# Top-k attention and an MLP on one core: the scores of the first batch one item further ahead and at another place of the slot

## The chip, the cores and the metric

The kernel runs on one core of a Trainium2 chip. The time is that of the device, in microseconds (us), from the first to the last instruction and what lies around them; the lower the better. PE is the matrix engine, DVE the vector engine, ACT the scalar engine, POOL the general one; SP issues DMAs. Each engine works through its own list of instructions in the order in which the program gave them out, and waits for others by semaphores.

## The reference, cut to what matters

```python
# q, k, v: (8, 8, 576, 64)  batch, heads, sequence, head size
scores = (1 / np.sqrt(64)) * q @ k.transpose(0, 1, 3, 2)
kth = np.partition(scores, -32, axis=-1)[..., -32:-31]     # the 32nd largest of a row
scores = np.where(scores >= kth, scores, -1e9)
p = np.exp(scores - scores.max(-1, keepdims=True))
x = (p / (p.sum(-1, keepdims=True) + 1e-9)) @ v            # -> (4608, 512)
h = x @ w_in                                               # (512, 2048)
y = gelu_exact(h) @ w_out                                  # (2048, 512)
```

## The kernel before, in words

**Items.** The attention is cut into items. An item is 128 query rows of two heads of one batch ("pair"), that is two rows of 576 scores in each of 128 partitions; two short items per batch take the last 64 queries of two pairs each. There are 144 items. The first 16 (`EARLY`) are the full tiles of batch 0, ordered so that four items (one tile of all four pairs) complete 128 tokens; batch 0 is "the first batch".

**Slots.** The program is written out by hand, with no scheduler: slot `n` gives out instructions for several items at different stages. Slots 0 to 17 are made by `early_slot(n)`, those from 18 on by the loop behind it. Before the slots come the transposes of pairs 0 to 2 with the scores of items 0 and 1. In slot `n` of `early_slot` there is, in the order in which it is given out:

- POOL adds the two halves of one block of weights (`weights_add`, L231). The weights arrive as 64-bit numbers, in 16 blocks, one per slot, and are turned into 32-bit ones in the kernel: ACT reads the high part in the middle of the slot before (`weights_size(u, 0)`, L211), ACT goes on with it at that slot's end (`weights_size(u, 1)`, L214, for the first blocks also L220; for the later ones DVE does that last step, L216).
- DVE compares the two halves of the rows of item n+1 (`larger`, L416); it is the first step of the top-k search and marks a slot's start on DVE below.
- `scores(n + 2)`: PE multiplies queries and keys: the last 64 keys into a bank of their own (`t_ps`, L343, or L357 for a short item), the 512 others into a tile of two banks (`s_ps`, L380 or L395). ACT scales and copies both to SBUF (L351 or L363, and L388 or L400).
- `attend(n - 2)`: PE multiplies the probabilities by the values (`o`, L638), ACT copies the product to `xT` (L656), PE spreads the reciprocals of the sums over the other half of the same bank (L651), and DVE multiplies `xT` by them (`copy_x`, L657).
- `top_k(n)`: DVE finds the 32nd largest of each row in six rounds of MAX8 and MATCH_REPLACE8. Rounds are given out in two parts, and `copy_x` stands between them: behind two rounds in the slots where a tile of 128 tokens is completed (`whole`), behind three in the others.
- `softmax(n - 1)`, twice, once per row: ACT L506 and L507.
- `transposes(n - 1)`: PE turns the probabilities over into a tile of two banks (`tp`, L568) and the last keys into another bank (`tp_t`, L542); ACT copies both (`pt`, L594 and L552).
- transposes of queries and keys of a later pair (`prep`, L291, copied by ACT in L296).
- `mlp(k)`: up to k pieces of the matmuls of the MLP are strewn between these. A piece is eight matmuls of `x @ w_in` (L721) or one of `g @ w_out` (L813), and every slot has a number of pieces (`left`); before slot 5 there are none, and dummy matmuls (`keep_busy`, L1092) stand there.
- At the end: `smaller` and `add_small` (POOL), `run_ends`, the rest of the search, `weights_size(u, 1)`, `run_gelus` (ACT, with a change of its table, L741), `threshold` (POOL, L486 and L487), `sum_up`.

`run_ends` copies a finished tile of y out of PSUM (L822) and stores it by a DMA of ACT's queue. It is so for the first five tiles of tokens only (`full_piece`).

**PSUM.** The eight banks are given out by tags. The tag that matters here is `pr`, two banks and one buffer: the scores and the transposed probabilities take turns in it. The two calls that do so:

```python
s_ps = pair_tile("s_ps", "l1" if second else "pr")      # in scores()
pr[0] = pair_tile("tp")                                 # in transposes(), tag "pr"
```

Of the kernel before, what the change touches and what calls it, by code (L numbers as in the profile page):

```python
# [14 lines left out]
def kernel(  # L15
# [30 lines left out]
    NP = H // 2  # L46
# [106 lines left out]
    EARLY = NP * NM  # L153
# [109 lines left out]
    def bank(name):  # L263

        tags = ("z",) if few[0] else ("z", "y2") if begun[0] else ("z", "y0", "y1", "y2")
        tag = tags[turn[0] % len(tags)]
        turn[0] += 1
        return ps.tile([P, 512], f32, tag=tag, bufs=1, name=name)
# [50 lines left out]
    def row(i, e):  # L319
        return S_of[i][:, e * S : (e + 1) * S]  # L320

    def spread(t, step, n):

        return bass.AP(tensor=t.tensor, offset=t.offset, ap=[list(t.ap[0]), [step, 2], [1, n]])

    def half(r, e):


        return slice((r ^ e) * TL, ((r ^ e) + 1) * TL)
# [5 lines left out]
    def pair_tile(name, tag="pr"):  # L335
        return ps.tile([P, 2, 512], f32, tag=tag, bufs=1, name=name)
# [31 lines left out]
    def scores(i, second=False):  # L368
        if i >= N or i in S_of:
            return  # L370
        pair, t = items[i]
        S_of[i] = s = work.tile([P, 2 * S], f32, tag="s", bufs=6, name="s")
        s_ps = pair_tile("s_ps", "l1" if second else "pr")
        if not few[0]:
            last_keys(i, bank("t_ps"))()
        if t < NM:
            q_t, kt = q_of[pair][:, t * P : (t + 1) * P], kt_of[pair]
            for e in range(2):
                rows = slice(e * D, (e + 1) * D)
                nc.tensor.matmul(  # L380
                    s_ps[:, e], lhsT=q_t[rows, :], rhs=kt[rows, 0:SM], start=True, stop=True
                )
            if i == 0:

                nc.scalar.activation(s[:, 0:SM], s_ps[:, 0], func=AF.Copy, scale=scale)
                nc.scalar.activation(s[:, S + TL :], s_ps[:, 1], func=AF.Copy, scale=scale)
                return
            nc.scalar.activation(spread(s, S + TL, SM), s_ps, func=AF.Copy, scale=scale)  # L388
        else:

            for r in range(2):
                kt = kt_of[pair + r]
                for e in range(2):
                    rows = slice(e * D, (e + 1) * D)
                    nc.tensor.matmul(  # L395
                        s_ps[half(r, e), r, :], lhsT=kt[rows, SM + P + e * TL : SM + P + (e + 1) * TL],
                        rhs=kt[rows, 0:SM], start=True, stop=True,
                    )
            s2 = s.rearrange("p (r n) -> p r n", r=2)
            nc.scalar.activation(s2[:, :, 0:SM], s_ps, func=AF.Copy, scale=scale)  # L400
# [4 lines left out]
    def paired(i):  # L405

        return PAIRED <= i < N and i not in SINGLE
# [19 lines left out]
    def smaller(i):  # L427

        if paired(i):
            both, top = lists_of[i][:, 1].bitcast(i32), lists_of[i][:, 0].bitcast(i32)  # L430
            nc.gpsimd.tensor_tensor(both, both, top, op=ALU.subtract)  # L431
# [63 lines left out]
    def add_small(i):  # L495
        if i < 0 or i >= N:
            return
        st = stat_of[i]
        nc.gpsimd.tensor_scalar(st["den"], st["den"], 1e-9, None, op0=ALU.add)  # L499

    def softmax(i, e):

        if i < 0 or i >= N:
            return
        st, s = stat_of[i], row(i, e)
        nc.scalar.activation(s, s, func=AF.Prelu, bias=st["neg"][:, e : e + 1], scale=1.0, alpha=STEEP)  # L506
        nc.scalar.activation(  # L507
            s, s, func=AF.Exp, bias=st["bias"][:, e : e + 1], scale=1.0,
            accum_out=st["den"][:, e : e + 1],
        )  # L510
# [94 lines left out]
    def copy_x():  # L605
        while copies:
            copies.pop()()
# [83 lines left out]
    for base in range(0, NT, RING):  # L691
        whole = [(0, 256), (256, 256)] if base else [(t * P, P) for t in range(NM)]
# [317 lines left out]
    def run_gelus():  # L1010
        while waiting:
            u = waiting.pop(0)
            if u in HELD:
                gelus(u - 2)
            gelus(u)
            if eager[0]:
                run_small(9)

    def run_ends():
        while ends:  # L1020
            ends.pop(0)()
# [23 lines left out]
    def mlp(n):  # L1045
        for _ in range(n):
            if done[0] >= len(pieces) or pieces[done[0]][0] > ready[0] or left[0] <= 0:
                return
            if not all(w in (known[0] or made) for w in pieces[done[0]][1]):
                return  # L1050
            pieces[done[0]][2]()
            done[0] += 1
            left[0] -= 1
            if eager[0]:
                run_gelus()
                run_small(9)
# [38 lines left out]
    for pair in range(3):  # L1095
        for piece in transpose_qk(pair, pair == 0):
            piece()
        if pair < 2:
            scores(pair)


    slots_of = [
# [33 lines left out]
    def early_slot(n):  # L1136

        left[0] = room_in(n) if n >= FIRST else 0
        begun[0] = n >= FIRST
        known[0] = set(made)  # L1140
        weights_add(unit_in(n))
        larger(n + 1)
        scores(n + 2)
        product = attend(n - 2)
        mlp(1)
        while dividing:
            dividing.pop()()
        searches = top_k(n, lambda: inverse(n - 1))
        whole = n - 2 < EARLY and (n - 1) % NP == 0
        for _ in range(2 if whole else 3):  # L1150
            next(searches)
        copy_x()
        ready[0] = n_tok[0]
        softmax(n - 1, 0)
        softmax(n - 1, 1)
        u = unit_in(n + 1)
        if u is not None:
            weights_size(u, 0)
        mlp(2)
        if n < FIRST:  # L1160
            keep_busy(6 if product else 12, ident)
        prep = prep_in.pop(n, [])
        for piece in prep[:1]:
            piece(None)
        tr = transposes(n - 1) if n - 1 < EARLY else []
        for x, piece in enumerate(tr):
            piece()
            if x == len(tr) - 1:
                known[0] = None
            mlp(1)  # L1170
        known[0] = None
        for piece in prep[1:]:
            piece(None)
            mlp(1)
        if n < FIRST:
            keep_busy(8, ident)
        smaller(n + 1)
        add_small(n - 1)
        mlp(left[0])
        run_ends()  # L1180
        for _ in searches:
            pass
        if u is not None:
            weights_size(u, 1)
        run_gelus()
        threshold(n)
        normalise(n - 1)
        sum_up(n + 2)
        run_small(6)
        next_loads(n)  # L1190
# [5 lines left out]
    for n in range(LAST_EARLY + 1, ahead):  # L1196

        left[0] = room_in(n)
        few[0] = n > START + 2
        eager[0] = n > N  # L1200
        larger(n + 1)
        for piece in squares_in.pop(n, []):
            piece()
        two = n >= SPREAD[1] and n % 2 == 0 and n + 3 < N and items[n + 3][1] < NM
        scores(n + 2, two)
        if two:
            scores(n + 3)
        product = attend(n - 3) if n - 3 >= EARLY else False
        copy_x()
        mlp(1)  # L1210
        if n % 2:
            run_gelus()
        tr = transposes(n - 2)
        if product and done[0] < len(pieces) and pieces[done[0]][0] > ready[0]:

            for piece in tr[:1]:
                piece(n + 2)
            tr, ready[0] = tr[1:], n_tok[0]
        mlp(1)
        softmax(n - 1, 0)  # L1220
        if n % 2:
            mlp(ODD)
        mlp(1)
        prep = prep_in.pop(n, [])
        for x, piece in enumerate(tr + prep[:1]):
            piece(n + 2)
            ready[0] = n_tok[0]
            if x == 2:
                break
            mlp(1)  # L1230
        ready[0] = n_tok[0]
        softmax(n - 1, 1)
        smaller(n + 1)
        add_small(n - 1)
        for piece in prep[1:]:
            piece(None)
            mlp(1)

        run_gelus()
        mlp(left[0])  # L1240
        run_ends()
        run_gelus()
        if n < N:
            for _ in top_k(n, lambda: inverse(n - 1)):
                pass
        else:
            inverse(n - 1)
        threshold(n)
        normalise(n - 1)
        sum_up(n + 2)  # L1250
        if n in sums_in:
            weight_sums(sums_in[n])
        run_small(6)
# [38 lines left out]
```

## Time and profile before

| | |
|---|---|
| median of 3 runs | 1562.04 us (1559.5 to 1562.1) |
| the profiled execution, its own time | 1561.84 us |
| its span, first to last instruction | 1559.1 us |
| PE busy | 1514.1 us, 97% |
| DVE busy | 1336.6 us, 86% |
| ACT busy | 1157.0 us, 74% |
| POOL busy | 1095.8 us, 70% |
| the chain that ended last | PE 72%, DVE 7%, POOL 6%, ACT 2% |

The shares are means over a span with different stages. The stage that the change touches, slots 0 to 17, ends at about 201 us of the span; what happens in it is read from windows and from the instructions in order of time, where a row gives start, duration, engine, line, and in brackets the idle time of the engine ahead of the instruction with what ended it. Two instructions of ACT that follow each other overlap a little, so the time that one takes out of ACT's day is best read from its start to the start of the next.

### The profile page before, as it was taken

To read this page: it belongs to the slowest core of one execution; us is meant where nothing else is said; L and a number is where in the kernel's file an instruction comes from. 1 tells how busy PE (TensorE), PEld (TensorE's weight loads), DVE (VectorE), ACT (ScalarE), POOL (GpSimd) and SP (SyncE) were. 2 spreads that over 40 slices of the span, in tenths; PEclk is the share of its full clock that TensorE was granted. 3 is DMA by queue.
4 is the path that set the end of the run, shared out by engine and by line. 5 is a ranking of instruction groups with operands and counts; after the bars stand their busy time and mean duration, and the time that the engine had idled before them with its cause. 6 is when DMAs were issued, how large, how long until landed. Compare 5 with 4: busy or idle time off the path is not lost.

```text
span 1559.1 us, 28536 instructions
## 1 busy us (share of the span) xinstructions
PE 1514.1 (97%) x9478; PEld 1178.0 (76%) x9478; DVE 1336.6 (86%) x4605; ACT 1157.0 (74%) x2030; POOL 1095.8 (70%) x1253
## 2 busy tenths in 40 slices
PE   8888999999999999999999999999999999999998
PEld 6765666667777778887777778788777777787887
DVE  8988889899989998998989997988998998888700
ACT  6988867677777777777777777777777778787720
POOL 4664555556687878776787877777778786876732
PEclk9999999999999999999999999999999999999999
DMA  6523210022101111011200111002210111000000
GB/s 178 159 84 104 85 39 8 8 38 39 24 14 26 36 31 30 1 30 38 39 23 16 30 32 45 1 17 38 37 24 19 28 30 32 15 1 15 8 14 14
DMA packets 184243, 56.37 MB, mean 36 GB/s; under 512 B 175008, under 2 KB 175584, under 8 KB 184096
## 3 DMA queue, kind: packets, MB, share of 16 engines
q1 hardware_dynamic: 180720, 52.23, 14.2%
q10 hardware_dynamic: 3152, 2.00, 0.4%
q8 instruction: 74, 1.21, 0.3%
q14 instruction: 73, 0.60, 0.1%
q0 software_dynamic: 224, 0.33, 0.1%
HBM read 45.08 MB, written 9.44 MB: 35 GB/s over the span
## 4 chain that ended last, share of the span: by engine, by line
PE 72%; DVE 7%; POOL 6%; ACT 2%; issue 1%; DVEq 0%; POOLq 0%
PE h_ps L721 26%; PE y_ps L874 15%; PE o L638 7%; PE tp L568 6%; PE s_ps L380 6%; PE y_ps L813 3%; PE seven L872 2%; DVE top L460 2%; POOL s L518 2%; DVE rest L463 2%; PE tp_t L343 1%; PE y_ps L836 1%; PE y_ps L839 1%; PE o L667 1%; PE tp_t L542 1%
## 5 line engine op out<-in xcount | busy, mean ns | idle before, releaser
L721 PE MATMUL h_ps<-xT,w_in_sb 128*128 128x256 f32 (+1 forms) x2688 | 529.3, 347 | 0.0
L721 PEld LDWEIGHTS h_ps<-xT,w_in_sb 128*128 128x128 f32 x2688 | 433.5, 191 | 64.6 <-issue 24.6
L460 DVE MAX8 top<-lists 128x8 f32<-128x288 f32 x798 | 323.6, 447 | 0.0
L518 POOL TENSOR_TENSOR s<-s,rden 128x1152 f32<-128x1152 f32 x128 | 269.1, 2102 | 0.3 <-DVE rden L493 0.3
L507 ACT ACTIVATE s<-s,bias 128x576 f32<-128x576 f32 x288 | 223.4, 776 | 12.0
L463 DVE MATCH_REPLACE8 lists<-top,lists 128x288 f32<-128x288 f32 x532 | 231.5, 443 | 0.0
L506 ACT ACTIVATE s<-s,neg 128x576 f32<-128x576 f32 x288 | 225.7, 784 | 4.0 <-POOL neg L486 4.0
L460 DVE MAX8 low<-lists 128x8 f32<-128x288 f32 x532 | 214.7, 445 | 0.0
L499 POOL TENSOR_SCALAR den<-den 128x2 f32<-128x2 f32 x144 | 31.4, 218 | 259.2 <-ACT s L507 255.4
L584 ACT COPY pt<-tp 128x1024 f32<-128x1024 f32 x128 | 130.0, 1016 | 101.8 <-PE tp L568 101.8
L431 POOL TENSOR_TENSOR lists<-lists 128x576 int32<-128x576 int32 x133 | 187.6, 1411 | 4.4
L423 POOL TENSOR_TENSOR lists<-s 128x576 int32<-128x576 int32 x133 | 187.0, 1406 | 0.0
L568 PE MATMUL tp<-ident,s 128*128 128x128 f32 x1152 | 152.7, 273 | 9.8 <-ACT s L507 9.8
L486 POOL TENSOR_SCALAR neg<-kth 128x2 f32<-128x2 f32 x133 | 84.9, 639 | 106.4 <-DVE kth L477 106.4
L638 PEld LDWEIGHTS o<-pt,raw_v 128*64 128x64 f32 x1440 | 93.0, 137 | 87.0 <-issue 45.3
L568 PEld LDWEIGHTS tp<-ident,s 128*128 128x128 f32 x1152 | 134.0, 141 | 28.9 <-ACT s L507 13.1
L638 PE MATMUL o<-pt,raw_v 128*64 128x256 f32 (+1 forms) x1440 | 154.7, 361 | 0.0
L388 ACT ACTIVATE s<-s_ps 128x1024 f32<-128x1024 f32 x127 | 124.9, 1026 | 22.5 <-PE s_ps L380 21.6
L380 PE MATMUL s_ps<-kt,qm 64*128 64x512 f32 x512 | 131.9, 625 | 4.3 <-ACT pt L584 2.9
L874 PE MATMUL y_ps<-w_out_sb,sum 128*128 128x256 f32 x448 | 133.3, 379 | 0.0
L493 DVE RECIPROCAL rden<-den 128x2 f32<-128x2 f32 x144 | 23.0, 160 | 120.8 <-POOL den L499 120.0
L463 DVE MATCH_REPLACE8 lists<-low,lists 128x288 f32<-128x288 f32 x266 | 115.8, 443 | 0.0
(168 smaller groups left out, 2744.8 us busy)
## 6 DMA issues: line engine op xcount, KB each, us to landing
raw_v<-in_v_dram SPq DMA_DIRECT2D x64, 128.0 KB, 2.3
w_out_sb<-in_moe_w_in_dram SPq DMA_DIRECT2D x14, 511.8 KB, 4.8
out_dram<-late SPq DMA_DIRECT2D x26, 256.0 KB, 2.1
raw_q<-in_q_dram SPq DMA_DIRECT2D x96, 64.0 KB, 2.0
raw_k<-in_k_dram SPq DMA_DIRECT2D x96, 64.0 KB, 2.0
w_out_sb<-in_moe_w_out_dram SPq DMA_DIRECT2D x10, 511.8 KB, 4.2
w_sum<-in_moe_w_out_dram SPq DMA_DIRECT2D x4, 511.8 KB, 5.6
raw_q<-in_q_dram SPq DMA_DIRECT2D x96, 8.0 KB, 1.8
```

The costliest lines, as they stand in the source:

```text
L380: nc.tensor.matmul(s_ps[:, e], lhsT=q_t[rows, :], rhs=kt[rows, 0:SM], start=True, stop=True)
L423: nc.gpsimd.tensor_tensor(t[:, 1].bitcast(i32), a.bitcast(i32), b.bitcast(i32), op=ALU.add)
L431: nc.gpsimd.tensor_tensor(both, both, top, op=ALU.subtract)
L460: nc.vector.max(x[:, e], src[:, e])
L463: nc.vector.match_replace(dst[:, e], x[:, e], src[:, e], LOWEST)
L506: nc.scalar.activation(s, s, func=AF.Prelu, bias=st["neg"][:, e : e + 1], scale=1.0, alpha=STEEP)
L507: nc.scalar.activation(s, s, func=AF.Exp, bias=st["bias"][:, e : e + 1], scale=1.0, accum_out=st["den"][:, e : e + 1],)
L518: nc.gpsimd.tensor_tensor(s, s, wide, op=ALU.mult)
L568: nc.tensor.transpose(tp[:, j * P : (j + 1) * P], s[:, first + j * P : first + (j + 1) * P], ident)
L638: nc.tensor.matmul(o[e * D : (e + 1) * D, 0:n], lhsT=vt[:, j, e, :], rhs=pt[:, e * NM + j if j < NM else 2 * NM, x], start=(j == 0), stop= ...
L721: nc.tensor.matmul(h_tile(u)[:, i, :], lhsT=w_in_sb[:, ko, f * P : (f + 1) * P], rhs=xT[:, ko, c0 : c0 + n], start=(ko == 0), stop=(ko == ...
L874: nc.tensor.matmul(acc[names][:, k], lhsT=lhsT, rhs=rhs, start=(j == 0 and k == 0), stop=(j == FT // 2 - 1 and k == 1),)
```

## The change

The scores are made one item further ahead and are given out late in the slot. `scores(2)` is given out before slot 0, and slot `n` makes `scores(n + 3)` behind the transposes and the pieces between them, instead of `scores(n + 2)` at the slot's head. `smaller` and `add_small` with one piece of the MLP stand ahead of it; in slots 0 to 4 the second run of dummy matmuls stands behind it. `copy_x` stands behind two rounds of the search in all early slots. `run_ends` moves from the end of the slot to behind the second softmax, in the early slots and in the main loop.

```diff
@@ before the slots
     for pair in range(3):
         for piece in transpose_qk(pair, pair == 0):
             piece()
-        if pair < 2:
-            scores(pair)
+        scores(pair)
@@ early_slot(n)
         larger(n + 1)
-        scores(n + 2)
         product = attend(n - 2)
         mlp(1)
         while dividing:
             dividing.pop()()
         searches = top_k(n, lambda: inverse(n - 1))
-        whole = n - 2 < EARLY and (n - 1) % NP == 0
-        for _ in range(2 if whole else 3):
+        for _ in range(2):
             next(searches)
         copy_x()
         ready[0] = n_tok[0]
         softmax(n - 1, 0)
         softmax(n - 1, 1)
+        run_ends()
         u = unit_in(n + 1)
         if u is not None:
             weights_size(u, 0)
...
         for piece in prep[1:]:
             piece(None)
             mlp(1)
+        smaller(n + 1)
+        add_small(n - 1)
+        mlp(1)
+        if n + 3 <= EARLY + 3:
+            scores(n + 3)
         if n < FIRST:
             keep_busy(8, ident)
-        smaller(n + 1)
-        add_small(n - 1)
         mlp(left[0])
-        run_ends()
         for _ in searches:
             pass
         if u is not None:
             weights_size(u, 1)
@@ the main loop
         ready[0] = n_tok[0]
         softmax(n - 1, 1)
+        run_ends()
         smaller(n + 1)
...
         run_gelus()
         mlp(left[0])
-        run_ends()
         run_gelus()
```

## The prediction

> **What bounds the kernel now.** I read the windows first, to see which engine is full in the stage that the change touches, then the instructions in order of time through that stage, and last the waits. In the windows the columns are the stretch, its length, the busy time of PE, weight loads, DVE, ACT and POOL, then the granted clock, the DMA share and GB/s.
>
> ```profile
> 40.00:60.00 20.00, 17.32 (x158) 13.38 (x159) 19.93 (x74) 19.77 (x32) 14.27 (x16) 1.00 0.57 161
> 80.00:100.00 20.00, 14.62 (x118) 10.24 (x114) 19.31 (x70) 17.55 (x28) 13.67 (x13) 0.91 0.28 106
> 140.00:160.00 20.00, 20.00 (x115) 10.24 (x113) 16.11 (x59) 16.80 (x28) 10.71 (x11) 0.96 0.18 43
> ```
>
> There are two stages. Up to about 100 us DVE is full, and between 40 and 60 ACT is too (19.77 of 20); PE has room, and part of its work there is dummy matmuls. From about 140 us on PE is full. Every later slot has its fixed share of MLP pieces and PE stays full, so a microsecond that slots 0 to 17 lose or win should reach the end whole. Here is ACT from slot 2 to slot 3, from one copy of `xT` to the next, and the starts of two slots on DVE:
>
> ```profile
> 34.16 0.24 ACT L656 COPY xT<-o 128x128 f32<-128x128 f32 x1
> ...
> 39.53 0.27 ACT L552 COPY pt<-tp_t 128x128 f32<-128x128 f32 x1
> 39.68 1.26 ACT L214 ACTIVATE w_in_sb<-w_sum,low 128x1024 int32<-128x1024 f32 x1
> 40.82 1.19 ACT L220 ACTIVATE w_sum<-w_sum 128x1024 int32<-128x1024 uint32 x1
> 41.87 0.29 ACT L351 ACTIVATE s<-t_ps 128x128 f32<-128x128 f32 x1
> 42.02 1.05 ACT L388 ACTIVATE s<-s_ps 128x1024 f32<-128x1024 f32 x1
> 42.93 0.30 ACT L656 COPY xT<-o 128x128 f32<-128x128 f32 x1
> ```
> ```profile
> 39.44 0.75 DVE L416 TENSOR_TENSOR lists<-s 128x576 f32<-128x576 f32 x1
> ...
> 48.49 0.75 DVE L416 TENSOR_TENSOR lists<-s 128x576 f32<-128x576 f32 x1
> ```
>
> ACT's round takes 42.93 − 34.16 = 8.77 us, and no row of it has a bracket, that is, ACT never waits; DVE's takes 48.49 − 39.44 = 9.05. ACT has 0.28 us to spare per slot. What the change does to ACT's list decides.
>
> **What the order of the lists becomes.** On PE almost nothing changes. The scores of item n+3 are given out at the end of slot n instead of at the head of slot n+1, and from slot 9 on the 6 or 7 pieces of a slot are all used up ahead of the new place: 1 + 2 before the transposes, 3 in them, 1 new. PE meets the scores where it met them before. In slots 0 to 4 they swap places with the dummy matmuls; in slots 5, 6 and 8, where the pieces wait for their weights, they pass one or two. POOL's and SP's lists keep their order: the scores issue no DMA, and `smaller` and `add_small` pass nothing of POOL's. `scores(2)` ahead of slot 0 is the old order too. These edits cost nothing by themselves.
>
> On ACT, however, the copies of the scores (L351, L388) pass `weights_size(u, 1)` (L214, in the first slots also L220) and the gelus. L388 needs `s_ps`, and `s_ps` lies in the buffer that L594 empties:
>
> ```profile
> 86.28 0.99 ACT L594 COPY pt<-tp 128x1024 f32<-128x1024 f32 x1
> 87.18 0.27 ACT L552 COPY pt<-tp_t 128x128 f32<-128x128 f32 x1
> 87.33 2.08 PE L380 MATMUL s_ps<-kt,qm 64*128 64x512 f32 x4 [1.04 <-ACT pt L594]
> ```
> ```profile
> 146.76 1.13 PE L380 MATMUL s_ps<-kt,qm 64*128 64x512 f32 x4
> ...
> 147.94 1.03 ACT L388 ACTIVATE s<-s_ps 128x1024 f32<-128x1024 f32 x1 [0.79 <-PE s_ps L380]
> ...
> 150.12 0.44 PE L651 MATMUL o<-ident,rden 128*64 128x128 f32 x4
> ```
>
> PE can start `s_ps` 0.15 us after ACT goes on from L594 (87.33 − 87.18), and L388 starts 1.18 us behind that (147.94 − 146.76). Before, L214 and L220 filled this time. After, only L552 and L351 do, 0.15 us each from start to start (39.68 − 39.53, 42.02 − 41.87).
>
> *Slots 1 to 4.* ACT newly waits 0.15 + 1.18 − 0.30 = 1.03 us per slot. Its round becomes 9.80 us, over DVE's 9.05, so ACT takes over as the bound: **4 × 1.03 = 4.1 us**. If DVE's round is taken as the old bound it is 4 × 0.75 = 3.0. I take the first, for ACT's hand-over to DVE was just in time when the MLP begins in slot 5: PE waits for ACT, and is done at 60.94 + 0.44 = 61.38 for DVE's L657 at 61.49.
>
> ```profile
> 60.59 0.30 ACT L656 COPY xT<-o 128x128 f32<-128x128 f32 x1
> ...
> 60.94 0.44 PE L651 MATMUL o<-ident,rden 128*64 128x128 f32 x4 [0.55 <-ACT xT L656]
> ...
> 61.49 0.29 DVE L657 TENSOR_TENSOR xT<-xT,o 128x128 f32<-128x128 f32 x1
> ```
>
> *Slot 0.* Item 3 needs the queries of its pair, which ACT copies at 21.59:
>
> ```profile
> 11.35 0.63 ACT L296 COPY qm<-tp_qk 128x512 f32<-128x512 f32 x1
> ...
> 13.63 1.02 ACT L388 ACTIVATE s<-s_ps 128x1024 f32<-128x1024 f32 x1 [0.79 <-PE s_ps L380]
> 21.59 0.60 ACT L296 COPY qm<-tp_qk 128x512 f32<-128x512 f32 x1
> ...
> 25.50 0.77 ACT L506 ACTIVATE s<-s,neg 128x576 f32<-128x576 f32 x1
> ```
>
> From such a copy to L388 it took 13.63 − 11.35 = 2.28, so L388 falls at 23.87. Behind it come its own 0.91 (42.93 − 42.02), then L214 and L220, 41.87 − 39.68 = 2.19, and the first softmax starts at 26.97 instead of 25.50: **1.5 us**.
>
> *Slots 5 to 7.* Where PE has pieces, ACT waited for `s_ps` already, as the 0.79 at 147.94 shows. The new wait of 1.03 replaces such a wait in part; I take 0.4 each, **1.2 us**, from −0.8 (one old wait goes and nothing comes) to 3.1 (all of it is new).
>
> *The three slots that end in gelus (8, 11, 15).*
>
> ```profile
> 97.04 0.26 ACT L552 COPY pt<-tp_t 128x128 f32<-128x128 f32 x1
> ...
> 102.77 0.33 ACT L656 COPY xT<-o 128x128 f32<-128x128 f32 x1
> ```
>
> ACT now takes 102.77 − 97.04 = 5.73 us from L552 to L656, for L214, a table load, four gelus and the two copies of the scores, without a wait. The new order has the same instructions and the wait of 1.03 ahead of L388. PE and DVE wait for this L656 already, so **3 × 1.0 = 3.1 us** (1.5 to 5.0; PE's pieces and the transposes of a pair can hold the scores up longer).
>
> *The other slots with pieces and a block of weights (9, 10, 12, 13, 14).* PE is full, and the question is whether ACT has L656 ready when PE comes to L651. L388 at 147.94, its 0.91, then L214's 1.14 (40.82 − 39.68) put L656 at 149.99; L651 follows by 0.35 (60.94 − 60.59), at 150.34 instead of 150.12: **5 × 0.2 = 1.0 us** (0 to 2.5).
>
> *The rest.* `copy_x` one round of the search earlier makes DVE wait at L657 instead of working on. ACT's round being the longer one, DVE stands later against ACT once, not in every slot, and the biases of the next softmax are still early: nothing. The copy of y now stands behind the softmaxes with its DMA issue; what it passes on ACT are copies that wait for PE anyway, and the next tile in its bank is two slots away: nothing, a few tenths either way.
>
> The sum is 4.1 + 1.5 + 1.2 + 3.1 + 1.0 = 10.9 us; with the bounds, 3.0 + 1.5 − 0.8 + 1.5 + 0 = 5.2 to 4.1 + 1.5 + 3.1 + 5.0 + 2.5 = 16.2. On the profiled execution, 1561.84 us, that is 1572.7; the median of the runs shown is 0.2 higher, so I say **1572.9 us**, from 1567.2 to 1578.2.
>
> **The rivals.** *The clock drops (slower still).* In slots 7 and 8 PE has few pieces; the window 80 to 100 was granted 0.91, and the four matmuls of `s_ps` took 2.08 us at 87.33 where they took 1.13 at 146.76. Longer slots leave longer gaps there. What that window lost, 0.09 × 20 = 1.8 us, may come twice more: 1572.9 + 3.6 = 1576.5. The Trainium skill ("TensorE: Matmul & The Clock Gate", HAM oscillation) has the rule behind it: idle gaps of more than about 3.4 us set the clock back to half. The 2.08 against 1.13 agrees with a half clock.
>
> *It is faster.* What the change takes away is a meeting of three engines at the slot's head:
>
> ```profile
> DVE xT L657 <- PE o L651: 11.5, 7, 3.4
> ...
> PE o L651 <- ACT xT L656: 6.0, 9, 1.6
> ```
>
> If ACT is through with L214 while PE still works, L656 starts at once and PE's 6.0 us at L651 go: 1562 − 6 = 1556 us; with DVE's 11.5 us too, 1550.5. It decides at L388 + L214 + the way from L656 to L651, 0.91 + 1.14 + 0.35 = 2.40 us, against what PE does between the start of L388 and L651, 150.12 − 147.94 = 2.18. That is close in slots 9 to 14; against it speak the gelus, and slots 1 to 4, where the one buffer makes ACT wait whatever PE does.
>
> *Half of it is hidden.* If the 5.6 us of slots 0 to 4 are absorbed, DVE and not ACT having held that stage, 5.3 remain: 1567.3.
>
> *Nothing changes.* PE's order being the same, the waits may only move: 1562.
>
> **How the numbers follow.** The forecast 0.52, the clock 0.14, half hidden 0.12, nothing 0.08, faster 0.14. The range takes in the forecast with its bounds, the clock and the half: from 1563.5 to 1578.5. Outside lie "faster" and most of "nothing". A measurement of this kernel can tell about 0.2%, 3.1 us, from no change: slower by more 0.78, within 0.08, faster by more 0.14.
>
> **What would show it.** In the changed kernel ACT waits about 1 us for `s_ps` ahead of L388 in each of slots 1 to 4, and its round there is 9.8 us; DVE has waits at L657 in those slots; the L656 of slot 5 comes about 5.6 us later than at 60.59, and slot 18 begins about 11 us later. From there both traces run in parallel. I am wrong if ACT's round stays at 8.8 us, if the loss does not grow from slot to slot, or if the main loop gives it back.

## The result: 1578.6 us against 1562.1, and the profile after

The changed kernel takes 1578.57 us (median of 4 runs, 1577.19 to 1580.1), the kernel before beside it 1562.07 (1559.5 to 1564.5): 16.5 us slower, a ratio of 1.0106 with the interval 1.0087 to 1.0125. Forecast were 1572.9 us and a range up to 1578.5: the direction was right, the size too small. The profiled execution took 1578.13 us with a span of 1576.3, that is 16.3 and 17.2 more than before.

The loss lies where it was expected. The rows are the copies of `xT` (ACT, L656) and the waits ahead of the scores in slots 2 and 3, where the quoted round of before was.

```profile
36.78 0.27 ACT L656 COPY xT<-o 128x128 f32<-128x128 f32 x1
...
42.19 0.25 ACT L552 COPY pt<-tp_t 128x128 f32<-128x128 f32 x1
42.34 0.26 ACT L351 ACTIVATE s<-t_ps 128x128 f32<-128x128 f32 x1
43.51 1.02 ACT L388 ACTIVATE s<-s_ps 128x1024 f32<-128x1024 f32 x1 [0.90 <-PE s_ps L380]
44.43 1.24 ACT L214 ACTIVATE w_in_sb<-w_sum,low 128x1024 int32<-128x1024 f32 x1
45.56 1.18 ACT L220 ACTIVATE w_sum<-w_sum 128x1024 int32<-128x1024 uint32 x1
46.76 0.27 ACT L656 COPY xT<-o 128x128 f32<-128x128 f32 x1
```

The round is 46.76 − 36.78 = 9.98 us instead of 8.77 (forecast 9.80). The bracket of 0.90 at L388 is the forecast wait. PE in the same slot:

```profile
42.33 1.13 PE L380 MATMUL s_ps<-kt,qm 64*128 64x512 f32 x4 [1.05 <-ACT pt L594]
43.39 2.05 PE L1092 MATMUL warm<-ident 128*128 128x128 f32 x16
45.37 1.31 PE L638 MATMUL o<-pt,raw_v 128*64 128x128 f32 x20
```

Two chains start at the copy of `pt`, and both end at L656: ACT's (L388, L214, L220, done at 45.56 + 1.18 = 46.74) and PE's (`s_ps`, 8 dummies in 16 rows, `o`, done at 45.37 + 1.31 = 46.68). Keep this pair in mind; the experiments turn on it. In the rows PE's ends last, by about 0.2 us: L656 starts 0.08 us behind the end of `o`, as it does in experiment 1 below, where it waits for `o` by its bracket; and ACT, whose instructions overlap, goes on from L220 after 1.20 us here (46.76 − 45.56), after 1.05 in the kernel before (41.87 − 40.82) and after 1.00 in experiment 6. ACT's chain alone would thus give about the forecast round of 9.80. The waits between 20 and 205 us (engine, tile, line, what it waits for, total, times, longest) have grown; the first two were 11.5 and 5.0 us before, 7 times each, and the third was 1.2:

```profile
DVE xT L657 <- PE o L651: 31.0, 14, 5.9
...
ACT s L388 <- PE s_ps L380: 11.7, 13, 1.8
...
ACT s L351 <- PE t_ps L343: 9.1, 7, 2.3
```

And the granted clock (the third number from the end) was lower than before in the stretches that follow:

```profile
40.00:60.00 20.00, 15.51 (x134) 12.06 (x134) 18.29 (x67) 17.96 (x30) 12.37 (x13) 1.00 0.37 121
80.00:100.00 20.00, 15.23 (x106) 11.54 (x106) 16.84 (x61) 14.97 (x25) 11.37 (x12) 0.83 0.46 136
100.00:120.00 20.00, 15.51 (x124) 13.09 (x121) 16.63 (x61) 18.58 (x31) 10.90 (x10) 0.91 0.30 106
140.00:160.00 20.00, 15.30 (x67) 8.14 (x65) 14.08 (x50) 15.58 (x24) 8.94 (x10) 0.74 0.23 86
```

Before, 80 to 100 had 0.91 and 140 to 160 had 0.96. DVE, with 19.93 of 20 us the fullest engine between 40 and 60 before, is down to 18.29: no engine is full in that stage any more, the chain around the buffer is the bound.

For an account by slots I take the start of the first L651 of every slot on PE (the spread of the reciprocals, which waits for L656). The loss of a slot is how much more one kernel than the other needs from there to the next slot's. The last column compares the two kernels with PE's gaps filled (experiments 8 and 9 below), where the clock takes little; 0.28 us of its first row lie ahead of slot 0 (see the starts named below).

| slots | forecast | changed − before | the same, gaps filled |
|---|---|---|---|
| 0 to 4 | 5.6 | 6.09 | 6.29 |
| 5 to 7 | 1.2 | 3.03 | 1.91 |
| 8, 11, 15 (gelus) | 3.1 | 4.80 | 4.27 |
| 9, 10, 12, 13, 14 | 1.0 | 1.36 | 1.65 |
| sum at slot 17 | 10.9 | 15.29 | 14.14 |

From there the traces run in parallel, 15.3 to 15.6 us apart (slot 18 starts on DVE with the lag that L651 of slot 17 has, so both are called the lag at slot 18). The last tile adds 1.6 us inside the span (experiment 10), and what lies around the span is 0.9 shorter: 15.3 + 0.3 + 1.6 − 0.9 = 16.3.

### The profile page after: what moved, and what is told of

It reads as the page before. It is cut to its first block, busy times and chain, and to the rows that moved or that the text cites. A ratio compares the mean times of both kernels' runs of the same rounds, so it can differ in the third digit from the quotient of the medians.

```text
span 1576.3 us, 28530 instructions
## 1 busy us (share of the span) xinstructions
PE 1524.2 (97%) x9478; PEld 1184.2 (75%) x9478; DVE 1336.0 (85%) x4605; ACT 1157.4 (73%) x2030; POOL 1097.7 (70%) x1253
## 4 chain that ended last, share of the span: by engine, by line
PE 72%; DVE 6%; POOL 6%; ACT 1%; issue 1%; SPq 0%; DMA 0%; DVEq 0%; POOLq 0%
PE h_ps L721 26%; PE y_ps L874 14%; PE o L638 7%; PE tp L568 6%; PE s_ps L380 6%; PE y_ps L813 3%; PE seven L872 2%; DVE top L460 2%; POOL s L518 2%; DVE rest L463 1%; PE tp_t L343 1%; PE y_ps L836 1%; PE y_ps L839 1%; PE o L667 1%; PE tp_t L542 1%
## 5 line engine op out<-in xcount | busy, mean ns | idle before, releaser
L388 ACT ACTIVATE s<-s_ps 128x1024 f32<-128x1024 f32 x127 | 124.8, 1025 | 32.2 <-PE s_ps L380 31.3
```

## The experiments

Times are medians; the kernel before had 1561.39, 1561.25 and 1561.17 us in the three sets of runs (1 to 4, 5 to 8, 9 to 12). The theory: the scores, made late, wait for a buffer that ACT empties, and ACT's weights and gelus queue behind that wait. The rivals: the other moves of the change, PE's order with the dummies, the clock. In kernels with added lines the line numbers shift by 1 to 5; the tiles' names tell which is which. The diffs are shortened. The profiled executions differ in their start, ahead of slot 0 and whatever the change: `t_ps` of item 2 (L343) starts at 15.95 us in the kernel before, at 16.00 in the changed one and between 15.5 and 16.3 in the others, but at 18.39 in experiment 1 and 18.71 in experiment 11. A lag below holds this difference too.

### Which part of the change costs it (1 to 4)

Experiment 1 gives ACT its weights ahead of the late scores; DVE's step L216 stays.

```diff
+        if u is not None:
+            weights_size(u, 1, "act")
         if n + 3 <= EARLY + 3:
             scores(n + 3)
...
-            weights_size(u, 1)
+            weights_size(u, 1, "dve")
```

> The changed kernel, but ACT's end of the weights (L214, early L220) stands ahead of the late scores again; DVE's step stays where it was. PE's list, copy_x and run_ends are those of the changed kernel. Theory A (the loss is ACT waiting for s_ps with nothing left to fill the time, and PE's clock falling in the gaps that this makes): the waits ahead of L388 in slots 1 to 4 go, the first softmax is back at about 25.5 us, the L656 of slot 5 at 60.6 to 61.2 instead of 66.7, no doubled matmuls in slots 6, 9 and 12, and the time is within 3 us of before (1560 to 1565). Rival B (it is the place of the scores on PE, or copy_x one round early, that costs): it stays at 1570 or more.

Measured: 1570.46 us, 1.0055 (1.0038 to 1.0071), where theory A had 1560 to 1565: the expectation missed. Nearly half of the loss goes, but none of it in slots 1 to 4. Slots 5, 6, 9, 10, 13 and 14 come to 0.2 us or less each, so there ACT's weights behind the scores were the cause; of the slots with gelus, 11 and 15 come to 0.28 and 0.45, and 8 keeps 1.41. Slots 1 to 4 lose as in the changed kernel, with a round of 67.52 − 57.55 = 9.97. ACT does not wait for `s_ps` there any more, and still waits, for PE's `o` (rows of PE, then of ACT, from slot 4 to slot 5):

```profile
66.13 1.31 PE L640 MATMUL o<-pt,raw_v 128*64 128x128 f32 x20
```
```profile
57.55 0.27 ACT L658 COPY xT<-o 128x128 f32<-128x128 f32 x1 [1.05 <-PE o L640]
...
65.43 1.01 ACT L390 ACTIVATE s<-s_ps 128x1024 f32<-128x1024 f32 x1
67.52 0.27 ACT L658 COPY xT<-o 128x128 f32<-128x128 f32 x1 [1.07 <-PE o L640]
```

The other chain of the pair, PE's, gives the same round by itself.

Experiment 2 leaves out the move of the scores (`scores(2)` goes back too) and keeps all others.

```diff
         larger(n + 1)
+        scores(n + 2)
...
-        if n + 3 <= EARLY + 3:
-            scores(n + 3)
```

> The changed kernel with the scores put back (item n+2, at the head of the slot); what remains of the change is copy_x behind two rounds everywhere, run_ends behind the second softmax, and smaller and add_small one step earlier. Theory A: these cost nothing, 1561 to 1564, DVE waits longer at L657 and is not later at slot 18 (about 201 us). Rival B: copy_x one round early makes DVE's slots longer, some 0.6 to 0.8 us in each of the 12 slots where it had three rounds, 1567 to 1572.

Measured: 1562.47 us, 1.0011 (1.0001 to 1.0021); slot 18 lies 0.76 us earlier than before. The scores are the whole loss.

Experiments 3 and 4 make them late in slots 0 to 4 alone, and from slot 5 on alone; elsewhere `scores(n + 2)` stands at the slot's head as before.

```diff
-        if n + 3 <= EARLY + 3:
+        if n < FIRST:                   # 3; 4 has: if FIRST <= n <= EARLY:
             scores(n + 3)
```

> The changed kernel with the scores late in slots 0 to 4 only; from slot 5 on they are those of item n+2 at the head again. Theory A: L656 of slot 5 at 66.7 as in the changed kernel, 6.1 us late, and from there the lag stays, 5 to 7 us at slot 18: 1567 to 1570. If PE's clock falls in slots 6, 9 and 12 only because of the late scores there, this kernel shows no more doubled matmuls than before. Rival C (DVE and not ACT bounds slots 1 to 4, the lag is won back later): 1562 to 1565.

> The changed kernel with the scores late from slot 5 on only; before that they stand at the head. Theory A: L656 of slot 5 at 60.6, then the lag grows as in the changed kernel by 9 to 10 us to slot 18, with doubled matmuls in slots 6, 9 and 12: 1570 to 1573. The two halves, this one and the one late in slots 0 to 4, add up to the whole 16.5 us. Rival C: the slots from 5 on lose only because the early ones came late; then this one is at 1562 to 1566.

Measured: 1567.64 us (1.0043, 1.0028 to 1.0058) and 1571.49 (1.0073, 1.0058 to 1.0088); at slot 18 5.17 and 11.77 us, together 16.9 against the 15.29 of the whole (by the medians 6.25 + 10.10 = 16.35 against 16.5). Both stages lose, and the later one, forecast at 5.3, loses the more.

### The two chains of slots 1 to 4 (5 to 7)

Experiment 5 puts dummies, the rest of the pieces and ACT's weights ahead of the scores, so that only DVE's step and the gelus stand behind them. Experiment 6 puts only the dummies ahead. Experiment 7 leaves the order, and gives the scores of these slots the other two banks, the dummies a single one.

```diff
# 5
-        if n + 3 <= EARLY + 3:
-            scores(n + 3)
         if n < FIRST:
             keep_busy(8, ident)
         mlp(left[0])
+        if u is not None:
+            weights_size(u, 1, "act")
+        if n + 3 <= EARLY + 3:
+            scores(n + 3)
# 6
         if n < FIRST:
             keep_busy(8, ident)
+        if n + 3 <= EARLY + 3:
+            scores(n + 3)
         mlp(left[0])
# 7
-            scores(n + 3)
+            scores(n + 3, n < FIRST)       # tag "l1", not "pr"
-            keep_busy(8, ident)
+            keep_busy(8, ident, True)      # one bank of its own
```

> The changed kernel with three things ahead of the late scores: the dummy matmuls of slots 0 to 4, the rest of the slot's pieces, and ACT's end of the weights; only the gelus still stand behind them. With the weights alone ahead the lag at slot 5 was 6.9 us, for PE then ran 16 dummy matmuls between s_ps and o and ACT waited for o. Theory A2 (two chains of equal length bind slots 1 to 4, ACT's and PE's over the dummies; both have to go): L656 of slot 5 back at 60.6 to 61.5, no lag from the pieces in slots 5, 6 and 8, in all 1561 to 1565. Rival B (looking one item further ahead costs by itself): a lag of 3 us or more in slots 0 to 8, 1566 or more.

> The changed kernel with only the dummy matmuls ahead of the late scores; ACT's list is that of the changed kernel. Theory A2: ACT's chain alone gives a round of 9.80 us in slots 1 to 4 (8.77 + 1.03) instead of 9.97, so the lag at slot 5 is still 5.3 to 5.6 us and the whole stays at 15 to 16 us over before, 1576 to 1578. If the dummies were the only cause: lag under 1 us at slot 5, 1571 or less.

> The changed kernel in its order, but the scores made in slots 0 to 4 lie in the two banks that the MLP uses later, not in those of the transposed probabilities, and the dummies behind them in single banks. s_ps then needs not wait for L594. Theory A2 (the one buffer is what both chains of slots 1 to 4 hang on): no wait ahead of L388 there, a round of 8.8 to 9.1 us, L656 of slot 5 at 62 to 63 (the 1.5 us of slot 0 stay), and the rest as in the changed kernel: 1572 to 1575. Rival (ACT's order itself costs, whatever the buffer): the round stays at 9.8 or more, 1577 to 1580.

The lag of 6.9 us that the expectation of 5 names for experiment 1 holds 2.4 us of that run's later start; its slots up to there lose 4.5.

Measured: 5 takes 1566.33 us (1.0031, 1.0019 to 1.0043). Its slots 0 to 4 lose nothing (0.2 us ahead of before, as its start is), as theory A2 had it; the time misses the expected 1561 to 1565, for slots 8 and 9, the gelus and what follows them, lose 1.81 and 2.08 us. 6 takes 1581.06 (1.0128, 1.0112 to 1.0143), slower than the change; its expectation, 1576 to 1578, missed. Part of it arises in slot 1, where PE waits 2.03 and 0.92 us and the 16 rows of dummies behind take 3.62 us instead of 1.95: at L651 of slot 2 the lag is 6.4 us, in the changed kernel 2.6. With the dummies ahead, `s_ps` starts later and ACT's chain is the longer one; it now waits for `t_ps` and for `s_ps`:

```profile
50.98 0.26 ACT L656 COPY xT<-o 128x128 f32<-128x128 f32 x1
...
57.30 0.28 ACT L351 ACTIVATE s<-t_ps 128x128 f32<-128x128 f32 x1 [0.65 <-PE t_ps L343]
58.37 1.03 ACT L388 ACTIVATE s<-s_ps 128x1024 f32<-128x1024 f32 x1 [0.79 <-PE s_ps L380]
...
61.39 0.26 ACT L656 COPY xT<-o 128x128 f32<-128x128 f32 x1
```

That is a round of 10.41. So in slots 1 to 4 ACT's weights ahead alone (1) win nothing, the dummies ahead alone (6) lose, since they lengthen ACT's chain, and both together (5) win all of it. 7 takes 1573.06 us (1.0073, 1.0058 to 1.0088), as expected: with a buffer of their own the late scores cost ACT no wait,

```profile
44.26 0.27 ACT L656 COPY xT<-o 128x128 f32<-128x128 f32 x1
...
49.64 0.27 ACT L552 COPY pt<-tp_t 128x128 f32<-128x128 f32 x1
49.80 0.29 ACT L351 ACTIVATE s<-t_ps 128x128 f32<-128x128 f32 x1
49.97 1.04 ACT L388 ACTIVATE s<-s_ps 128x1024 f32<-128x1024 f32 x1
...
53.11 0.27 ACT L656 COPY xT<-o 128x128 f32<-128x128 f32 x1
```

and the round is 8.85, with L656 again 0.08 us behind PE's `o`. The one buffer is what binds both chains.

### The clock (8 and 9)

In the changed kernel PE takes far longer for the same matmuls behind short gaps (slots 5, 6 and 9):

```profile
72.04 1.95 PE L721 MATMUL h_ps<-xT,w_in_sb 128*128 128x128 f32 x16
...
80.35 0.66 PE L568 MATMUL tp<-ident,s 128*128 128x128 f32 x4 [1.18 <-ACT s L507]
```
```profile
81.92 0.66 PE L568 MATMUL tp<-ident,s 128*128 128x128 f32 x4 [0.91 <-ACT s L507]
...
82.52 3.49 PE L721 MATMUL y_ps<-xT,w_in_sb 128*128 128x128 f32 x16
```
```profile
113.43 0.69 PE L651 MATMUL o<-ident,rden 128*64 128x128 f32 x4 [2.58 <-ACT xT L656]
114.06 3.35 PE L721 MATMUL h_ps<-xT,w_in_sb 128*128 128x128 f32 x16
```

Experiment 8 repeats some matmuls, with the same operands and result, where PE waited; experiment 9 does the same to the kernel before.

```diff
-            return [lambda: turn_over(pr[0][:, 0], 0), ...]
+            # row 0 three times for items 5, 6, 7, row 1 three times for item 10
-                    for e in range(2):                    # spread_out, L651
+                    for e in (0, 1) * (4 if i in (4, 5) else 1):
-            for j in range(NJ):                           # o, L638
+            for j in list(range(NJ)) * {7: 2, 10: 3}.get(i, 1):
+            # and the last keys' matmul (L343) four times for item 10
```

> The changed kernel with matmuls of PE done again, with the same result, where it waited in slots 6 to 9, 11 and 12: the transposes of a row up to three times, the spreading of the sums four times, the product of items 7 and 10 two and three times, the last keys of item 10 four times. It adds work and no wait is meant to go. Theory D (in slots 6, 9 and 12 the clock fell to half after gaps, which made the lag grow by 1.6, 1.3 and about 2 us more than ACT's order): the matmuls there are at full speed, the granted clock 80 to 160 is 0.95 or more, 3 to 5 us are won, 1573 to 1576. If the clock's fall is only beside the path: no change or slower, 1578 or more.

> The kernel before, with the same repeated matmuls as in the filled version of the changed kernel. Theory (the clock's loss is mostly the change's own: its gaps in slots 6, 9 and 12): before lost at most 0.09 x 20 + 0.05 x 20 + 0.04 x 20 = 3.6 us to the clock between 80 and 160, and the fills win 1 to 3 of it: 1559 to 1561 us, less than the 4.9 us that they won in the changed kernel. Rival (the fills help either kernel alike, and the clock says nothing about the change): 4.9 us here too, 1556.5. Other rival (the repeats lengthen the way of an item, and nothing is won): 1562 or more.

Measured: 8 takes 1573.64 us (1.0074, 1.0057 to 1.0091), 4.9 less than the change. The same 16 matmuls, and the windows:

```profile
82.80 1.95 PE L726 MATMUL y_ps<-xT,w_in_sb 128*128 128x128 f32 x16
```
```profile
80.00:100.00 20.00, 16.37 (x150) 12.71 (x149) 18.25 (x65) 17.43 (x30) 12.82 (x13) 1.00 0.47 136
...
140.00:160.00 20.00, 18.07 (x126) 10.14 (x123) 13.14 (x48) 15.93 (x24) 8.95 (x9) 0.91 0.15 54
```

9 takes 1559.51 us, 1.7 less than before (0.9985, 0.9977 to 0.9994), within its expectation; by slot 18 it has won 2.98 us. This corrects a reading that 8 alone would suggest: the kernel before loses to the clock too. The change's own share is the difference, 4.14 − 2.98 = 1.2 us at slot 18 (1.4 if the executions are set to the same start), or 16.5 − (1573.64 − 1559.51) = 2.4 by the medians. Since 8 still had a window of 0.91, it is rather a little more than 1.2. Most of the loss is in the order, not in the clock.

### The tail, and what is left (10 to 12)

10 is 9 with 12 dummy matmuls (24 in the rows) on PE ahead of the last tile's first piece; 11 is 10 with all moves of the change but the scores; 12 is 7 with the repeats.

```diff
     while done[0] < len(pieces):
+        if done[0] == len(pieces) - 7:
+            keep_busy(12, ident)
         mlp(1)
```

> The kernel before with the same repeats, and 12 dummy matmuls on PE ahead of the last tile's first piece, where PE idles 2.43 us for POOL at 1548.49. Where the granted clock holds through this gap the time is that of the version without them within 0.4 us; where it falls, as in the profiled run of the changed kernel (0.80 against 1.00 in these 5 us, 1.6 us longer), 1 to 1.6 us are won. I expect 0.5 on the median: 1558.5 to 1560.5 us.

> The scores at the slot's head as before; the other moves of the change (copy_x behind two rounds in all early slots, the copy of y behind the second softmax, the small sums ahead of a piece), the repeats and the 12 dummies at the end. Theory (these moves alone are worth 0 to 0.8 us, as slot 18 lay 0.76 earlier with them): 1558 to 1560 us, the fastest of the kernels. Rival (they are worth nothing, or cost 0.5): the same as the kernel before with repeats and dummies, or 0.5 more.

> The changed kernel with both cures: the scores of slots 0 to 4 in the other two banks, which won 5.5 us, and the repeated matmuls where PE waited, which won 4.9. Theory (the shared buffer in slots 1 to 4 and the clock in slots 6, 9 and 12 are two separate losses): 1578.6 - 5.5 - 4.9 = 1568.2, 1567 to 1570 us. Rival (they are one loss, the clock falls because the early slots run late): no less than the better of the two alone, 1572 to 1574.

Measured, 10: 1557.95 us (0.9976, 0.9966 to 0.9985), the fastest kernel here and faster than both (1558.5 to 1560.5 had been expected). Before the last tile PE waits 2.43 us for POOL in every kernel without these dummies. Here are the twelve matmuls behind this wait in the changed kernel, in the kernel before and in 9:

```profile
1564.10 2.07 PE L872 MATMUL seven<-w_sum,g 128*128 128x256 f32 x4 [2.43 <-POOL g L758]
1565.96 2.63 PE L874 MATMUL y_ps<-w_out_sb,g 128*128 128x256 f32 x8
```
```profile
1548.49 1.13 PE L872 MATMUL seven<-w_sum,g 128*128 128x256 f32 x4 [2.43 <-POOL g L758]
1549.46 1.89 PE L874 MATMUL y_ps<-w_out_sb,g 128*128 128x256 f32 x8
```
```profile
1545.59 1.23 PE L877 MATMUL seven<-w_sum,g 128*128 128x256 f32 x4 [2.43 <-POOL g L763]
1546.62 3.52 PE L879 MATMUL y_ps<-w_out_sb,g 128*128 128x256 f32 x8
```

The same gap costs 1.6 to 1.7 us in one execution and nothing in another; of the twelve profiled executions that leave it open, eight show such a slow stretch behind it and four, the kernel before among them, do not. With it filled the twelve matmuls take 1.05 and 1.89 us, and 7 of 8 runs lie between 1557.69 and 1558.12; without, they spread from 1557.52 to 1561.0 mostly near 1557.8 or 1559.5. How often the changed kernel pays this, run by run, was not counted. Against 9 the intervals overlap, so that the medians' gain of 1.6 is likely but not shown.

11: 1558.64 us (0.9985, 0.9976 to 0.9993), not faster than 10. Its profile starts 2.7 us later than that of 9, ahead of slot 0, and in the slots has one loss against it, 0.63 us in slot 5, which experiment 2 has too (0.64): DVE, held up at L657 behind two rounds instead of three, comes with `copy_x` 1.34 us after L651 there and not 0.55, and PE waits for it:

```profile
63.62 0.44 PE L656 MATMUL o<-ident,rden 128*64 128x128 f32 x4 [0.53 <-ACT xT L661]
63.99 0.94 PE L726 MATMUL h_ps<-xT,w_in_sb 128*128 128x128 f32 x6
65.29 1.38 PE L726 MATMUL h_ps<-xT,w_in_sb 128*128 128x128 f32 x10 [0.37 <-DVE xT L662]
```

12: 1568.31 us (1.0043, 1.0031 to 1.0055), where 1568.2 was expected. The shared buffer and the clock are two separate losses, and both are cured. What is left against 9 is 8.8 us, 8.57 at slot 18: 1.57 in slots 0 to 4, 2.35 in 5 to 7, 4.29 in the three gelu slots, 0.34 in the others. The windows from 80 to 160 have the full clock in both kernels, and the other moves do not cost this (experiments 2 and 11), so it is the order that the late scores make; that it lies in ACT's list is read from the rows below.

## Why the prediction fell short, step by step

**ACT's list decides: right from slot 5 on, half right before.** Experiments 1 to 4 show it: only the scores' move costs, and putting ACT's weights ahead takes away the loss of slots 6, 9, 10, 13 and 14 and most of that of 11 and 15, but not that of slots 1 to 4, where PE's list gives the same round. Slower was given 0.78, and the signs held: the waits at L388 and L657, the loss growing from slot to slot, slot 18 later by 15.3 (forecast 11), parallel traces after.

**Slots 0 to 4: 6.09 instead of 5.6.** The first softmax starts where it was put:

```profile
26.97 0.77 ACT L506 ACTIVATE s<-s,neg 128x576 f32<-128x576 f32 x1
```

Slots 2 to 4 lose 1.13 to 1.16 us each instead of 1.03. The failed step is "These edits cost nothing by themselves", said of PE's order with the dummies. The swap built a second chain through the same buffer, which lets L656 start about 0.2 us later than ACT's would (0.08 us behind the end of `o` at 46.68). In the sum it is worth only 0.1 us per slot, the rest of it running beside ACT's chain, but it costs the whole 1.1 us per slot as soon as ACT's is cured (experiment 1).

**Slots 5 to 7: 3.03 instead of 1.2, at the full clock 1.9 to 2.4.** The failed step is "replaces such a wait in part; I take 0.4 each". ACT waits twice there, for `t_ps` behind PE's pieces and then for `s_ps`, and L214 and L220, which filled the first wait before, now come behind both. In slot 5 of the kernel before and of the changed one:

```profile
69.06 0.28 ACT L351 ACTIVATE s<-t_ps 128x128 f32<-128x128 f32 x1 [0.42 <-PE t_ps L343]
70.13 1.03 ACT L388 ACTIVATE s<-s_ps 128x1024 f32<-128x1024 f32 x1 [0.79 <-PE s_ps L380]
```
```profile
72.25 0.27 ACT L552 COPY pt<-tp_t 128x128 f32<-128x128 f32 x1
74.25 0.28 ACT L351 ACTIVATE s<-t_ps 128x128 f32<-128x128 f32 x1 [1.74 <-PE t_ps L343]
75.32 1.02 ACT L388 ACTIVATE s<-s_ps 128x1024 f32<-128x1024 f32 x1 [0.79 <-PE s_ps L380]
```

**The gelu slots: 4.80 instead of 3.1, at the full clock 1.18, 1.49 and 1.60.** The same step: only the wait for `s_ps` was priced. In slot 15 ACT waits 0.67 + 0.76 = 1.43 us ahead of its copies of the scores, where it waited for neither before, and PE waits 2.51 where it waited 0.92 (the last two rows, before and after):

```profile
193.21 0.28 ACT L363 ACTIVATE s<-t_ps 128x128 f32<-128x128 f32 x1 [0.67 <-PE t_ps L357]
194.24 1.02 ACT L400 ACTIVATE s<-s_ps 128x1024 f32<-128x1024 f32 x1 [0.76 <-PE s_ps L395]
```
```profile
183.70 0.44 PE L651 MATMUL o<-ident,rden 128*64 128x128 f32 x4 [0.92 <-ACT xT L656]
```
```profile
198.97 0.69 PE L651 MATMUL o<-ident,rden 128*64 128x128 f32 x4 [2.51 <-ACT xT L656]
```

The working named this ("PE's pieces and the transposes of a pair can hold the scores up longer") and put it into the bound, not the value.

**The other slots: right in kind.** Slots 10, 13 and 14 lost 0.14, 0.20 and 0.16 where 0.2 was forecast. Slot 9's 0.97 is the clock: 0.14 with the gaps filled.

**The clock: a term, not a rival.** It stood beside the sum with a chance of 0.14 and 3.6 us on top. Waits of ACT that PE shares come in the same slots as PE's thin work, so it had to come with the forecast. Its net share is 1.2 to 2.4 us, less than the 3.6 feared, since before it already cost about 3 us. "Nothing", "half hidden" and "faster" are refuted by the main result, and the last by its own point of decision: PE waited for ACT's L656 longer (7.4 us between 20 and 205 us against 6.0), not shorter.

**The rest at nothing: nearly.** All other moves cost −0.8 to 0.6 us at slot 18 (experiments 2 and 11, the latter without its later start). `copy_x` alone is at fault for 0.6, in kernels where nothing else delays PE; in the changed kernel L657 again follows 0.55 us after L651 in slot 5, and nothing shows.

In sum: 10.9 forecast; some 2.1 more from the order (5.6, 1.2, 3.1 and 1.0 became 6.0, 2.35, 4.3 and 0.3, sum 13.0; the 6.0 is 6.29 without the 0.28 ahead of slot 0); 2.3 from the clock up to slot 17, as the rest to 15.3; 1.0 from the main loop and the tail. That makes 16.3. The bound of 16.2 held for the slots, but the range had no room for the tail. The tail's 1.6 us is chance as far as the traces tell; the 2.1 and the 2.3 are what the working had wrong.

## What to carry to other kernels

When an operation on an in-order engine is moved behind a producer that may be late, price every wait ahead of it, not just the last one, and ask what used to fill that time. Where one buffer is shared, follow all chains that leave it, on every engine: a chain that ends together with another adds almost nothing to the time, and keeps the whole of its cost when the other is cured. And where a change opens gaps on the matrix engine, the granted clock belongs into the forecast itself, for both kernels.

## What was not expected of the hardware

The clock fell behind gaps much shorter than I had looked for: two of 1.18 and 0.91 us with 0.66 us of work between them, and then 16 matmuls took 3.49 us instead of 1.95. The Trainium skill ("TensorE: Matmul & The Clock Gate", HAM oscillation) speaks of idle gaps of more than about 3.4 us. The slow stretches here do not need one: the matmuls at 87.33 us that the prediction quotes stood behind a gap of 1.04, and only two gaps of the profiled executions are over 3.4, one of 3.97 us in experiment 7 (ahead of L813 at 143.43) and one of 3.41 us in experiment 5, behind which 16 matmuls took 3.78:

```profile
105.37 0.69 PE L653 MATMUL o<-ident,rden 128*64 128x128 f32 x4 [3.41 <-ACT xT L658]
106.00 3.78 PE L723 MATMUL h_ps<-xT,w_in_sb 128*128 128x128 f32 x16
```

And it is no fixed threshold: the gap of 2.43 us in the tail was followed by a slow stretch in eight of the twelve profiled executions that leave it open, and not in the other four.
